# Output product of a SoLU layer after talking-heads attention: seven block products per pair of token tiles for eight

## The chip, the core and the metric

The kernel runs on one core of one Trainium2 chip. The metric is the device time of one execution in microseconds (us); lower is better. The engines are TensorE (PE, with its weight loads PEld), VectorE (DVE), ScalarE (ACT), GpSimd (POOL) and SyncE (SP, which here only issues DMAs). Each engine works through its own instructions in order and waits on semaphores for the others.

## The reference

Attention with mixing across heads gives `x` of 1792 tokens by 768; the layer behind it is what the change touches:

```python
def _moe_ref(x, w_in, w_out, g_ln):          # x 1792x768, w_in 768x1024, w_out 1024x768
    h = x @ w_in
    e = np.exp(h - np.max(h, axis=-1, keepdims=True))
    solu = h * (e / (np.sum(e, axis=-1, keepdims=True) + 1e-09))
    mu = np.mean(solu, axis=-1, keepdims=True)
    var = np.mean((solu - mu) ** 2, axis=-1, keepdims=True)
    ln = (solu - mu) / np.sqrt(var + 1e-06) * g_ln
    return (ln @ w_out).astype(np.float32)
```

`w_in` and `w_out` arrive as 64-bit floats.

## The kernel before

The first 440 us are attention; the change leaves them alone. Every product in f32 accuracy is made of f16 parts: a value is scaled and split into a high and a low f16 part, and a product is three f16 products, high by high, high by low and low by high.

The second stage works on 14 tiles of 128 tokens (`NT`), in the order of `TURNS`. For a tile `t`:

- `hidden` (line 984) makes `x @ w_in` on PE in 36 matmuls of 512 columns, into one of three pairs of PSUM banks. Tile `t` needs the banks of tile `t - 3`, which are free after `solu_product` of that tile. Tile 0 is made at the end of attention.
- The SoLU chain runs on DVE, ACT and POOL: `solu_max` (DVE, line 1508, reads PSUM), `solu_exp` (ACT, 1519), `solu_guard` and `solu_invert` (DVE, 1530 and 1533, one column), `solu_product` (DVE, 1536, reads PSUM and SBUF), `ln_mean` (DVE, 1547), `ln_square` (ACT, 1552), `ln_var` (DVE, 1558), `ln_root` (POOL, 1563, one column), `ln_newton` (DVE, four small steps, 1568 to 1578), `ln_apply` (POOL, 1584, 1024 columns), `ln_hi` (ACT, 1590) and `ln_lo` (POOL, 1594).
- `turn` (line 1598) turns each half of the layer norm's rows by a DMA transpose on SP, from SBUF to SBUF, so that tokens lie along the columns.
- `project` (line 1609) multiplies the turned tile with `wo_h` and `wo_l`, in two halves of 384 output columns with 8 x 3 matmuls each, 48 in all. `emit` (ACT, 1621) scales each half out of PSUM, and SP stores it (1765).

`w_out` is prepared beside this. Its eight blocks of 128 rows are fetched as 64-bit words (`fetch_w_out`), made f32 by `convert_steps` (DVE 898, 904, 909 and 914, ACT 901, POOL 917) and their largest value found (ACT 1478). When all eight are there, one factor for all is worked out (DVE, ending in `gs_wo`, line 1490), and each block is split: `w_out_hi` on ACT (line 360) and `w_out_lo` on DVE (line 365).

The order on each engine is set by `Plan`: each task has engines with costs, tasks that it follows, a due time and rings of buffers, and a list scheduler takes what is ready and due first. For `w_out` block `kc` the due time is `9.0 * kc`, and `project` of a tile is due eleven tiles after its `hidden` (`LAG`). So one `project` stands between `hidden` of tile 12 and of tile 13, and all others behind the last `hidden`.

Of the kernel before, what the change touches and what calls it, by code (L numbers as in the profile page):

```python
# [240 lines left out]
def kernel(  # L241
# [1159 lines left out]
    with tc.manual_schedule():  # L1401
# [43 lines left out]
        junk = wt_p.tile([128, DFF], F32, name="junk")  # L1445
# [154 lines left out]
        ENDS = [[0, DM // 2, DM] if t < NT - 1 else [0, 2 * DM // 3, DM] for t in range(NT)]  # L1600

        def project(t, n, kcs):
            c0, c1 = ENDS[t][n : n + 2]
            if kcs[0] == 0:
                y = (ps_x, ps_y)[n].tile([128, 512], F32, tag="x", name=f"y{n}_{t}")
                ys[t, n] = y[:, 0 : c1 - c0]
            for kc in kcs:
# [8 lines left out]

        def emit(t, n):
            if n == 0:
                outs[t] = h_p.tile([128, DM], F32, tag="o", name=f"o_{t}")
# [67 lines left out]
        for t in range(NT):  # L1687
# [33 lines left out]
            for i, z in enumerate("hl"):  # L1721
                add(
                    ("zT", t, z),
                    one(turn, t, z),
                    {"sp": 1.4},
                    after=[("zl" if z == "h" else "zo", t)],
                    behind=[("zT", t - 1, z)] if t else [],
                    due=T + 9.5 + 2 * i,
                    ring="t" + z,
                    until=[("zP", t, 0, KFF - 1), ("zP", t, 1, KFF - 1)],  # L1730
                    dma=(16, 262, 16.4),
                )
            T = 7.75 * (t + LAG)
            for n in range(2):
                parts = [[kc] for kc in range(KFF)] if t == 0 else [list(range(KFF))]
                before = [("zP", t - 1, n, KFF - 1)] if t else []
                for j, kcs in enumerate(parts):
                    add(
                        ("zP", t, n, kcs[-1]),
                        one(project, t, n, kcs),  # L1740
                        {"pe": (ENDS[t][n + 1] - ENDS[t][n]) / 384 * 0.488 * len(kcs)},
                        after=[("zT", t, "h"), ("zT", t, "l")] + [("zL", kc) for kc in kcs],
                        behind=before,
                        due=T + (3.9 * n if t else 0.9 * j + 0.45 * n),
                        ring=None if j else "XY"[n],
                        until=[("zE", t, n)],
                    )
# [55 lines left out]
```

## Time and profile before

| | |
|---|---|
| three timed runs | 650.59, 653.63, 655.91 us; median 653.63 us |
| span of the profiled execution | 657.9 us |
| PE busy | 632.8 us, 96% of the span |
| DVE busy | 475.1 us, 72% |
| ACT busy | 451.0 us, 69% |
| POOL busy | 280.1 us, 43% |
| matmuls of `project`, line 1609 | 672, from 536.6 us to the last start at 653.4 us |

The profile is one execution; its span of 657.9 us is the only time that it has of its own, and lies 4.3 us above the median of the timed runs. A matmul's duration in it contains the time in which it overlaps with its neighbours, so what a row of matmuls costs is read from the distance of their starts. Times in the trace are microseconds from the start of the span; "idle before" is how long the engine waited before an instruction, with the instruction that ended the wait.

### The profile page before, as it was taken

The numbers are of one execution on the slowest core, as the hardware profiler recorded it, in microseconds if no ns is written. First come the engines' busy times: TensorE is split into PE (matmuls) and PEld (weight loads), VectorE is DVE, ScalarE is ACT, GpSimd is POOL, SyncE is SP. The second block draws the span as 40 slices with busy tenths as digits, with TensorE's granted clock in tenths as the row PEclk, the third lists the DMA queues.
The fourth block names the chain that finished last, engine by engine and source line by source line (L and its number), as shares of the span: only waits on it lengthen the run. The fifth ranks groups of instructions, "written<-read, shape, count | busy, mean of one in ns | idle before, by whom it ended". The sixth has DMA issues, their size and how long they took to land.

```text
span 657.9 us, 17741 instructions
## 1 busy us (share of the span) xinstructions
PE 632.8 (96%) x6660; PEld 433.7 (66%) x6660; DVE 475.1 (72%) x1314; ACT 451.0 (69%) x981; POOL 280.1 (43%) x427
## 2 busy tenths in 40 slices
PE   6889999999999999999899999999999999999997
PEld 6647767777767778778677777774444455666664
DVE  5769998879997689997699999849889896100000
ACT  4679888989888898988799997725455576311111
POOL 2025683235844254593254246404666846300000
PEclk9779999999999999999899999999999999999999
DMA  9037578467677448788746763019964422541211
GB/s 242 12 133 229 178 152 178 156 196 221 204 185 169 150 140 236 234 175 206 219 154 221 214 224 119 3 41 295 186 160 112 97 48 57 113 113 51 64 55 48
DMA packets 114029, 98.53 MB, mean 150 GB/s; under 512 B 69604, under 2 KB 104600, under 8 KB 113944
## 3 DMA queue, kind: packets, MB, share of 16 engines
q1 hardware_dynamic: 108120, 83.62, 45.8%
q0 software_dynamic: 4416, 12.40, 6.9%
q10 hardware_dynamic: 1408, 1.38, 0.8%
q8 instruction: 52, 0.85, 0.5%
q14 instruction: 33, 0.27, 0.1%
HBM read 33.24 MB, written 9.63 MB: 65 GB/s over the span
## 4 chain that ended last, share of the span: by engine, by line
PE 64%; DVE 17%; ACT 7%; DMA 4%; issue 3%; POOL 2%; SPq 1%; ACTq 0%; DVEq 0%; POOLq 0%
PE y L1609 17%; PE po L766 15%; PE ps_h L984 12%; PE px L815 7%; PE ps L644 6%; PE pm L711 6%; DVE dead L721 4%; DVE s L661 3%; ACT e L737 3%; ACT s L656 2%; DMA raw_q<-in_q_dram 2%; DVE hl_k L365 1%; ACT p_t L369 1%; DMA sr<-s 1%; DMA cv_wi<-in_moe_w_in_dram 1%
## 5 line engine op out<-in xcount | busy, mean ns | idle before, releaser
L766 PE MATMUL po<-wr,e 128*112 128x120 f32 x1440 | 176.0, 273 | 6.4 <-POOL wr L758 4.9
L766 PEld LDWEIGHTS po<-wr,e 128*112 128x112 f32 x1440 | 156.8, 178 | 36.8 <-POOL wr L758 15.9
L758 POOL TENSOR_SCALAR wr<-wq,sm 128x120 f32<-128x120 f32 x180 | 77.1, 436 | 186.1 <-DVE sm L752 90.6
L737 ACT ACTIVATE e<-pm,nb,c_exp 128x448 f32<-128x448 f32 x180 | 131.4, 734 | 19.6 <-DVE dead L721 10.2
L721 DVE TENSOR_SCALAR_CACHE_REDUCE dead<-pm,c_nexp 128x448 f16<-128x448 f32 x180 | 121.7, 676 | 14.1 <-PE pm L711 10.1
L661 DVE SCALAR_TENSOR_TENSOR s<-ps,s 120x448 f16<-120x448 f32 (+1 forms) x192 | 112.2, 615 | 16.1 <-ACT s L656 13.8
L369 ACT COPY p_t<-po 112x480 f32<-112x480 f32 x180 | 108.2, 625 | 13.7 <-PE po L766 12.3
L656 ACT ACTIVATE s<-ps 120x448 f16<-120x448 f32 (+1 forms) x192 | 97.3, 552 | 18.1 <-PE ps L644 17.5
L815 PE MATMUL px<-p_t,raw_v 112*64 112x120 f32 (+3 forms) x1632 | 86.8, 259 | 0.8 <-ACT e L737 0.7
L815 PEld LDWEIGHTS px<-p_t,raw_v 112*64 112x64 f32 x1632 | 76.1, 137 | 16.0 <-issue 11.4
L984 PE MATMUL ps_h<-wi,xf 128*128 128x512 f16 x396 | 86.0, 379 | 0.2 <-DVE u L1536 0.2
L644 PE MATMUL ps<-k,q 64*64 64x448 f16 (+2 forms) x1008 | 79.7, 359 | 2.2 <-DVE s L661 1.5
L1609 PE MATMUL y<-wo_h,lth 128*128 128x384 f16 (+2 forms) x224 | 73.0, 326 | 0.0
L1609 PE MATMUL y<-wo_l,lth 128*128 128x384 f16 (+2 forms) x224 | 73.0, 326 | 0.0
L1609 PE MATMUL y<-wo_h,ltl 128*128 128x384 f16 (+2 forms) x224 | 73.0, 326 | 0.0
L984 PEld LDWEIGHTS <-xf 128*128 128x128 f16 x396 | 38.8, 98 | 46.8 <-issue 0.4
L1621 ACT ACTIVATE o<-y,c_out 128x384 f32<-128x384 f32 (+2 forms) x28 | 16.2, 579 | 72.7 <-PE y L1609 72.7
L1609 PEld LDWEIGHTS <-lth 128*128 128x128 f16 x448 | 43.8, 98 | 29.3
L711 PE MATMUL pm<-sr,wp_hi 64*64 64x448 f16 x720 | 57.1, 363 | 4.4 <-DMA sr<-s 2.4
L644 PEld LDWEIGHTS <-q 64*64 64x64 f16 (+2 forms) x1008 | 34.7, 107 | 24.4 <-issue 8.0
L1594 POOL TENSOR_TENSOR ll<-u,lh 128x1024 f16<-128x1024 f32 x14 | 31.4, 2245 | 15.1 <-ACT lh L1590 9.0
L737 ACT ACTIVATION_READ_ACCUMULATOR e<-pm,nb,c_exp 128x1 f32 x180 | 37.6, 209 | 0.0
(182 smaller groups left out, 800.1 us busy)
## 6 DMA issues: line engine op xcount, KB each, us to landing
sr<-s SPq DMA_DIRECT2D x176, 210.0 KB
cv_wi<-in_moe_w_in_dram SPq DMA_DIRECT2D x24, 256.0 KB
cv_wo<-in_moe_w_out_dram SPq DMA_DIRECT2D x8, 768.0 KB
raw_k<-in_k_dram POOLq DMA_DIRECT2D x18, 224.0 KB, 3.7
raw_q<-in_q_dram POOLq DMA_DIRECT2D x18, 224.0 KB, 5.4
raw_v<-in_v_dram POOLq DMA_DIRECT2D x18, 224.0 KB, 3.8
xh<-xsh SPq DMA_DIRECT2D x9, 224.0 KB
xl<-xsl SPq DMA_DIRECT2D x9, 224.0 KB
```

The lines of the kernel that those rows point to most:

```text
L369: nc.scalar.copy(out=out, in_=in_)
L644: nc.tensor.matmul(sps[b, c, h + e][lo:hi], q2[b, g][rows, 2 * j + x, i0 + lo : i0 + hi], k1[b, g][rows, 2 * j + y], start=(a == 0), stop= ...
L656: nc.scalar.activation(out=s_t[b, c][0 : y.shape[0], h, 0], in_=y, func=AF.Copy, scale=2.0**-E_S)
L661: nc.vector.scalar_tensor_tensor(out=t[:, h, 1], in0=y, scalar=2.0**-E_S, in1=t[:, h, 0], op0=ALU.mult, op1=ALU.subtract)
L711: nc.tensor.matmul(pmx[b, u + i][64 * e : 64 * e + 64, 0:S], w[rows], sr[b, u][rows, e, z], start=(a == 0), stop=(a == 2),)
L721: nc.vector.tensor_scalar(out=dead, in0=pmx[b, u][:, 0:S], scalar1=c_nexp[0:UK, b : b + 1], scalar2=None, op0=ALU.mult, op1=ALU.min, accum ...
L737: nc.scalar.activation(out=ee[b, u], in_=pmx.pop((b, u))[:, 0:S], func=AF.Exp, bias=nbs.pop((b, u)), scale=c_exp[0:UK, b : b + 1], accum_o ...
L758: ENG[eng].tensor_scalar(out=w, in0=wq[0:UK, 0 : H * UN], scalar1=sm, scalar2=1.0, op0=ALU.mult, op1=ALU.mult)
L766: nc.tensor.matmul(ps[:, c * 120 : (c + 1) * 120], e[:, c * CP : (c + 1) * CP], w, start=True, stop=True)
L815: nc.tensor.matmul(xps[b, blk, g][e * 64 : e * 64 + 64, i, cut], raws["v", b, p][:, e, c * D : (c + 1) * D], next(x for y, x in block_view ...
L984: nc.tensor.matmul(ps[:, n], xx[:, kc, o : o + 128], ww[:, kc, n * 512 : (n + 1) * 512], start=(kc == 0 and a == 0), stop=(kc == KDM - 1 a ...
L1609: nc.tensor.matmul(ys[t, n], lts[t, x][:, kc], w[:, kc, c0:c1], start=(kc == 0 and a == 0), stop=(kc == KFF - 1 and a == 2),)
```

## The change

One level of Strassen's algorithm on the product with `w_out`. Two token tiles form a pair: with the turned rows of a pair as a 2 by 2 of blocks (two tiles by two halves of the 1024 inner rows) and `w_out` as a 2 by 2 (two halves of the rows by two halves of the columns), seven block products replace eight. The form with shared sums is used (Winograd's): four sums of blocks on each side.

- `w_out`: all blocks are first scaled in place (`w_out_scale`), four sums of 384 columns are made for each of four pairs of blocks (`w_out_sum`), and what is split is 20 pieces instead of 8: the eight blocks, four double sums (`tt`, 768 columns) and eight single ones (384 columns). `w_out_lo` becomes a plain subtraction (line 1510) that the scheduler may put on DVE or POOL, and so do the sums. Block `kc` is due at `7.0 * kc`, and the fetches have four buffers for two.
- Layer norm: `ln_store` writes both halves of a tile's rows to DRAM, and `turn` transposes them from DRAM.
- Pair 0 is projected plainly (`project` with `i == 0`, 4 steps of 24 matmuls). For pairs 1 to 6, high and low parts are added up again to f32 (`pair_whole`, line 1660, two of 1024 columns), four sums are made (`pair_sum`, 1673, four of 512 columns), and split again (`part_hi` on ACT, 1678, and `part_lo`, 1510, two of 1024 columns each). `project` then has 7 steps of 12 matmuls of 384 columns. Steps 0 to 2 read the turned tiles, steps 3 to 6 the split sums.
- `emit` leaves ACT for the pairs, except step 0: DVE adds each block product from PSUM to what is there (line 1755), nine instructions a pair.
- All 14 `hidden` come before the first step of `project`.

```diff
-        lt_p = ctx.enter_context(tc.tile_pool(name="lt", bufs=9))
+        lt_p = ctx.enter_context(tc.tile_pool(name="lt", bufs=2))
+        sz_p = ctx.enter_context(tc.tile_pool(name="sz", bufs=2))
...
-        LAG = 11
+        ln_dr = [dram.tile([NT, 128, DFF], F16, name=f"ln_{z}") for z in "hl"]
...
-        def w_out_lo(kc):
-            split_lo(wo_l[:, kc], wo_raw[kc // 4][:, kc % 4], gs_wo[:, kc : kc + 1], wo_h[:, kc])
+        def w_out_scale(kc, eng):
+            x, s = raw_of(kc), gs_wo[:, kc : kc + 1]
+            if eng == "act":
+                nc.scalar.activation(out=x, in_=x, func=AF.Copy, scale=s)
+            else:
+                ENG[eng].tensor_scalar(out=x, in0=x, scalar1=s, scalar2=1.0, op0=ALU.mult, op1=ALU.mult)
+
+        def minus(eng, out, x, y):
+            ENG[eng].tensor_tensor(out=out, in0=x, in1=y, op=ALU.subtract)
...
+            out, x, y = ((t[:, 0], b12, b11), (t[:, 1], b22, t[:, 0]), (b21, b21, t[:, 1]), (b12, b22, b12))[i]
+            minus(eng, out, x, y)
...
+        def w_out_hi(k):
+            x, hi, _ = w_out_views(k)
+            nc.scalar.copy(out=hi, in_=x)
+
+        def w_out_lo(k, eng):
+            x, hi, lo = w_out_views(k)
+            minus(eng, lo, x, hi)
...
+        def ln_store(t, z, e):
+            QUEUE[e].dma_start(out=ln_dr["hl".index(z)][t], in_=lns[t, z])
+
+        def turn(i, t, z):
+            if i not in lts:
+                lts[i] = lt_p.tile([128, 2, 2, KFF, 128], F16, tag="lt", name=f"lt_{i}")
+            z = "hl".index(z)
+            nc.sync.dma_start_transpose(out=lts[i][:, z, t], in_=ln_dr[z][2 * i + t])
...
+            h, l = (lts[i][:, z, t].rearrange("p k f -> p (k f)") for z in range(2))
+            ENG[eng].tensor_tensor(
+                out=xs[i][:, 2 * t : 2 * t + 2].rearrange("p n f -> p (n f)"), in0=h, in1=l, op=ALU.add
+            )
...
+        def part_lo(i, t, eng):
+            hi, lo = (szs[i][:, z, 2 * t : 2 * t + 2] for z in range(2))
+            minus(eng, lo, xs[i][:, 2 * t : 2 * t + 2], hi)
...
+            for k in range(KH):
+                wh, wl = factor(j, k)
+                for a, (z, w) in enumerate(((0, wh), (0, wl), (1, wh))):
                     nc.tensor.matmul(
...
+                        ys[i, j],
+                        operand(i, j, z, k),
+                        w,
+                        start=(k == 0 and a == 0),
+                        stop=(k == KH - 1 and a == 2),
...
+                3: lambda: [(py, py), (px, px)],
+                4: lambda: [(c(1, 0), py), (c(1, 1), px)],
...
+            for dst, x in work[j]():
+                nc.vector.scalar_tensor_tensor(out=dst, in0=y, scalar=c_out, in1=x, op0=ALU.mult, op1=ALU.add)
...
-            due = 9.0 * kc
+            due = 7.0 * kc
...
+                    {"dve": 0.48, "pool": 0.95},
...
+                    {"dve": 1.15, "pool": 2.2},
```

The order on DVE just behind the factor of `w_out` (`gs_wo`), before. `u_8522` is the SoLU of tile 11, `wo_l` the low parts of `w_out`:

```order
L1490 TENSOR_SCALAR gs_wo<-g_sb,p_wo 128x8
L1491 TENSOR_SCALAR c_out<-p_wo 128x1
L1558 TENSOR_SCALAR v_8517<-sq_8462,ch 128x1
L1547 TENSOR_SCALAR nmu_8519<-su_8468 128x1
L1508 TENSOR_SCALAR u_8522,nb_8523<-ps_h_7620,ch 128x1024
L365 SCALAR_TENSOR_TENSOR wo_l<-wo_7704,gs_wo,wo_h 128x768 x3
L1568 TENSOR_SCALAR z_8535<-y_8525,v_8517 128x1
```

The same place after; `u_8383`, `u_8465` and `u_8524` are tiles 9, 10 and 11, and `tt` is a sum of blocks of `w_out`:

```order
L1493 TENSOR_SCALAR gs_wo<-g_sb,p_wo 128x8
L1494 TENSOR_SCALAR c_out<-p_wo 128x1
L1577 RECIPROCAL sm_8394<-sm_8394 128x1
L1580 SCALAR_TENSOR_TENSOR u_8383,su_8457<-ps_h_7315,sm_8394,u_8383 128x1024
L1591 TENSOR_SCALAR nmu_8462<-su_8457 128x1
L1552 TENSOR_SCALAR u_8465,nb_8466<-ps_h_7622,ch 128x1024
L1510 TENSOR_TENSOR wo_l<-wo_7710,wo_h 128x768
L1510 TENSOR_TENSOR wo_l<-wo_8009,wo_h 128x768
L1510 TENSOR_TENSOR wo_l<-wo_7710,wo_h 128x768
L1602 TENSOR_SCALAR v_8482<-sq_8478,ch 128x1
L1510 TENSOR_TENSOR tt_8484<-wo_7710 128x384
```

The factor stands one `solu_max` and two `solu_product` earlier in the queue, and what follows it is a longer list: between it and the first split sums of pair 1, DVE has 10 subtractions of 768 columns, 16 of 384, one addition of 1024 and four of 512, beside the chains of tiles 9 to 13.

The order on POOL at the same place, before (`ll` is `ln_lo`, `u` by `rs,nm` is `ln_apply`, `y` by `half_p` is `ln_root`):

```order
L1594 TENSOR_TENSOR ll_8435<-u_8205,lh_8384 128x1024
L1584 TENSOR_SCALAR u_8308<-u_8308,rs_8426,nm_8430 128x1024
L1594 TENSOR_TENSOR ll_8458<-u_8308,lh_8448 128x1024
L1563 TENSOR_TENSOR y_8525<-v_8517,half_p 128x1
L1584 TENSOR_SCALAR u_8432<-u_8432,rs_8538,nm_8540 128x1024
```

After, `u_8314` being tile 8 and `u_8383` tile 9:

```order
L1628 TENSOR_SCALAR u_8314<-u_8314,rs_8402,nm_8404 128x1024
L1507 TENSOR_SCALAR wo_8009<-wo_8009,gs_wo 128x768
L1507 TENSOR_SCALAR wo_7710<-wo_7710,gs_wo 128x768
L1640 TENSOR_TENSOR ll_8475<-u_8314,lh_8468 128x1024
L1607 TENSOR_TENSOR y_8528<-v_8482,half_p 128x1
L1628 TENSOR_SCALAR u_8383<-u_8383,rs_8538,nm_8542 128x1024
L1510 TENSOR_TENSOR tt_8484<-wo_8009,tt_8484 128x384
L1510 TENSOR_TENSOR wo_l<-wo_7710,wo_h 128x768
L1640 TENSOR_TENSOR ll_8563<-u_8383,lh_8548 128x1024
```

Into the chain of the tiles on POOL come six scalings of 768 columns, six sums of 384, two low parts of 768 and two of 384, and one `pair_whole` of 1024 columns. The `ln_root` of tile 13 stands behind all of these, and behind `ln_lo` of tiles 8 to 12.

The order on DVE where the first split sums of pair 1 are made, after (`xs` are the pair's f32 blocks and sums, `sz` the split ones, `u_8747` is tile 13; none of this is in the kernel before):

```order
L1673 TENSOR_TENSOR xs_8825<-xs_8825 128x512
L1602 TENSOR_SCALAR v_8861<-sq_8840,ch 128x1
L1673 TENSOR_TENSOR xs_8825<-xs_8825 128x512 x3
L1612 TENSOR_SCALAR z_8887<-y_8882,v_8861 128x1
...
L1622 TENSOR_SCALAR nm_8893<-nmu_8838,rs_8891 128x1
L1510 TENSOR_TENSOR sz_8867<-xs_8825,sz_8867 128x1024
L1755 SCALAR_TENSOR_TENSOR o_8912<-y_1_8869,c_out,xs_8825 128x384
L1510 TENSOR_TENSOR sz_8867<-xs_8825,sz_8867 128x1024
L1755 SCALAR_TENSOR_TENSOR xs_8825<-y_2_8897,c_out,xs_8825 128x384
```

The last `sz` row here is what PE's step 3 of pair 1 waits for; the Newton steps of tile 13, which need POOL's `ln_root`, stand ahead of it.

## Rows read from the trace of the kernel before

**Rows 1.** The page, part 1: busy time, share of the span, instructions.
```profile
PE 632.8 (96%) x6660; PEld 433.7 (66%) x6660; DVE 475.1 (72%) x1314; ACT 451.0 (69%) x981; POOL 280.1 (43%) x427
```

**Rows 2.** Timeline of PE: start us, us, engine, line, operation, count [idle before].
```profile
458.26 70.09 PE L984 MATMUL ps_h<-wi,xf 128*128 128x512 f16 x324
...
528.80 7.93 PE L984 MATMUL ps_h<-wi,xf 128*128 128x512 f16 x36 [0.22 <-DVE u L1536]
...
544.36 7.93 PE L984 MATMUL ps_h<-wi,xf 128*128 128x512 f16 x36
```

**Rows 3.** The chain that ended last, its end: start us, us, what.
```profile
527.45 1.30 DVE u L1536 x2
528.80 7.93 PE ps_h L984 x36
536.73 7.80 PE y L1609 x48
544.53 7.77 PE ps_h L984 x36
552.30 101.41 PE y L1609 x624
```

**Rows 4.** Busy time by stretch: length, PE, PEld, DVE, ACT, POOL, PEclk, DMA, GB/s.
```profile
444.40:532.30 87.90, 87.68 (x408) 39.86 (x407) 77.00 (x165) 48.45 (x75) 55.92 (x35) 1.00 0.69 166
532.30:553.00 20.70, 20.70 (x111) 10.67 (x110) 17.09 (x38) 14.51 (x20) 12.03 (x8) 1.00 0.24 49
```

**Rows 5.** Timeline of DVE, four places.
```profile
457.46 2.37 DVE L909 TENSOR_SCALAR cv_wo<-cv_wo 128x768 uint32<-128x768 uint32 x1
...
502.26 1.28 DVE L1536 SCALAR_TENSOR_TENSOR u<-ps_h,sm,u 128x1024 f32<-128x1024 f32 x1
...
532.20 0.23 DVE L1490 TENSOR_SCALAR gs_wo<-g_sb,p_wo 128x8 f32<-128x8 f32 x1
...
533.78 2.87 DVE L365 SCALAR_TENSOR_TENSOR wo_l<-wo,gs_wo,wo_h 128x768 f16<-128x768 f32 x3
...
537.50 5.50 DVE L365 SCALAR_TENSOR_TENSOR wo_l<-wo,gs_wo,wo_h 128x768 f16<-128x768 f32 x5
```

**Rows 6.** Timeline of POOL, at those places and later.
```profile
457.17 2.23 POOL L1594 TENSOR_TENSOR ll<-u,lh 128x1024 f16<-128x1024 f32 x1 [1.32 <-ACT lh L1590]
...
461.21 1.85 POOL L917 TENSOR_TENSOR wo<-cv_wo 128x768 f32<-128x768 f32 x1
...
525.68 1.20 POOL L1584 TENSOR_SCALAR u<-u,rs,nm 128x1024 f32<-128x1024 f32 x1
528.04 2.14 POOL L1594 TENSOR_TENSOR ll<-u,lh 128x1024 f16<-128x1024 f32 x1 [1.16 <-ACT lh L1590]
...
537.76 3.51 POOL L1584 TENSOR_SCALAR u<-u,rs,nm 128x1024 f32<-128x1024 f32 x1 [4.53 <-DVE nm L1578]
...
561.46 0.55 POOL L1563 TENSOR_TENSOR y<-v,half_p 128x1 f32<-128x1 f32 x1 [2.07 <-DVE v L1558]
```

**Rows 7.** Groups by line: duration ns min/median/max, first and last start (SPq: time of issue).
```profile
L909 DVE TENSOR_SCALAR cv_wo<-cv_wo x8: 549/566/2373, 449.7 to 518.9; 128x768 uint32<-128x768 uint32 x8
L1508 DVE TENSOR_SCALAR_CACHE_REDUCE u<-ps_h,ch x14: 1268/1274/1284, 444.4 to 553.3; 128x1024 f32<-128x1024 f32 x14
L1536 DVE SCALAR_TENSOR_TENSOR u<-ps_h,sm,u x14: 1283/1284/1286, 447.5 to 558.3; 128x1024 f32<-128x1024 f32 x14
...
L1598 SPq DMA_TRANSPOSE lth<-lh x14: 1232/1233/2027, 461.8 to 583.4; - x14
```

**Rows 8.** Timeline of DVE: the small steps of one tile.
```profile
557.00 0.27 DVE L1568 TENSOR_SCALAR z<-y,v 128x1 f32<-128x1 f32 x1 [1.37 <-POOL y L1563]
557.31 0.15 DVE L1571 TENSOR_SCALAR z<-z 128x1 f32<-128x1 f32 x1
557.50 0.27 DVE L1574 TENSOR_SCALAR rs<-z,ch,y 128x1 f32<-128x1 f32 x1
557.80 0.21 DVE L1578 TENSOR_SCALAR nm<-nmu,rs 128x1 f32<-128x1 f32 x1
557.93 0.14 DVE L1530 TENSOR_SCALAR sm<-sm 128x1 f32<-128x1 f32 x1
558.11 0.16 DVE L1533 RECIPROCAL sm<-sm 128x1 f32<-128x1 f32 x1
```

**Rows 9.** Busy time by stretch near the start (columns as in rows 4).
```profile
8.00:16.00 8.00, 4.22 (x80) 3.74 (x74) 4.30 (x12) 3.78 (x8) 0.00 (x0) 1.00 1.14 256
16.00:24.00 8.00, 7.33 (x62) 5.97 (x64) 4.68 (x14) 4.78 (x12) 0.00 (x0) 0.57 0.16 41
```

More of the change, by code (lines that the diff above doesn't have):

```diff
@@ L1444 @@
         half_p = wt_p.tile([128, 1], F32, name="half_p")
[L1445 removed]
+        junk = wt_p.tile([128, DFF], F16, name="junk")
         wo_raw, wo_steps = [], {}
@@ new lines, in pair_sum, with part_hi @@
+        def pair_sum(i, j, eng):
+            a11, a12, a21, a22 = (xs[i][:, n] for n in range(4))
+            out, x, y, op = (
+                (a22, a21, a22, ALU.add),
+                (a21, a11, a21, ALU.subtract),
+                (a11, a22, a11, ALU.subtract),
+                (a12, a12, a11, ALU.subtract),
+            )[j]
+            ENG[eng].tensor_tensor(out=out, in0=x, in1=y, op=op)
+        def part_hi(i, t):
+            if i not in szs:
+                szs[i] = sz_p.tile([128, 9 * FH], F16, tag="sz", name=f"sz_{i}")[:, 0 : 8 * FH].rearrange("p (z n f) -> p z n f", z=2, n=4)
+            nc.scalar.copy(out=szs[i][:, 0, 2 * t : 2 * t + 2], in_=xs[i][:, 2 * t : 2 * t + 2])
@@ L1720 @@
                 prev = [(n, t)]
-            for i, z in enumerate("hl"):
+            for z, n, d in (("h", "zl", 9.3), ("l", "zo", 11.5)):
                 add(
[L1723 to L1731, printed above, removed]
-                )
@@ L1733 @@
[L1733 to L1737, printed above, removed]
-                    add(
[L1739 to L1746, printed above, removed]
-                    )
-                    before = [("zP", t, n, kcs[-1])]
-                add(
-                    ("zE", t, n),
-                    one(emit, t, n),
-                    {"act": (ENDS[t][n + 1] - ENDS[t][n]) / 384 * 0.35 + 0.15},
-                    after=before,
-                    behind=[("zE", t, n - 1)] if n else [("zE", t - 1, 1)] if t else [],
-                    due=T + 4 + 4 * n,
-                    ring=None if n else "o",
-                    until=[("zS", t, 1, i) for i in range(len(stores(t, slice(0, DM))))],
-                )
-                if n == 0 and t < NT - 1:
-                    continue
-                cut = slice(*ENDS[t][n : n + 2]) if t == NT - 1 else slice(0, DM)
-                for i, (_, d, rows) in enumerate(stores(t, cut)):
-                    add(
-                        ("zS", t, n, i),
-                        lambda e, d=d, rows=rows, t=t, cut=cut: nc.sync.dma_start(out=d, in_=outs[t][rows, cut]),
-                        {"sp": 0.6},
-                        after=[("zE", t, n)],
-                        due=T + 8.5 + 0.1 * i,
@@ new lines @@
+                    ("zS", t, z),
+                    lambda e, t=t, z=z: ln_store(t, z, e),
+                    {"sp": 0.6},
+                    after=[(n, t)],
+                    behind=[("zS", t - 1, z)] if t else [],
+                    due=T + d,
+                    dma=(16, 262, 18.5),
+                )
+        NPP = NT // 2
+        STEPS = [(0, j) for j in range(4)] + [(i, j) for i in range(1, NPP) for j in range(7)]
+        chunks = lambda t: range(len(stores(t, slice(0, DM))))
```

254 lines of the change are left out of this document (220 added, 34 removed).

## Prediction

> **What bounds the kernel now.** I read the busy times first: PE has 96% of the span, DVE 72%, ACT 69%, POOL 43% [rows 1]. Where an engine is that full, the next view is its timeline in the stage that the change touches. From 458.3 us `hidden` of tiles 3 to 11 runs without a gap (324 matmuls, so one tile's 36 take 7.77 us), then tile 12 from 528.80, one `project`, tile 13 from 544.36 [rows 2]. The chain that ended last says the rest: 48 matmuls of `project` take 7.80 us, and from 552.30 the other 624 run 101.41 us without a break to 653.7 [rows 3]. So 672 matmuls of 384 columns cost 109.2 us, 0.1625 us each, and 4.2 us pass from the last of them to the end of the span. PE sets the end.
>
> But the chain also steps aside to DVE: `solu_product` of tile 9 at 527.45 precedes `hidden` of tile 12, which waited 0.22 us for it [rows 2, 3]. DVE is busy 77.0 of the 87.9 us up to the factor of `w_out` at 532.2, and POOL 55.9 [rows 4]. PE is full because DVE is just fast enough, and in this stage the change gives DVE and POOL more work.
>
> **What PE saves.** After the change `project` has 4 steps of 24 matmuls and 42 of 12, 600 for 672: 72 times 0.1625, or 11.7 us. If PE never waits, it leaves `hidden` at 544.4 (without the 7.8 us of `project` now in between), ends pair 0 at 560.0 (96 matmuls, 15.6 us), and reaches step 3 of pair 1 at 565.8 (three steps of 1.95). Behind that start lie 39 steps, 76.1 us, and the end of 4.2 us: 646.1 against 657.9.
>
> **What must be there for step 3 of pair 1.** This is the first step that reads split sums. Before, nothing of the kind existed: `project` of tile 0 needed only turned rows eleven tiles old. Now the end is the time D at which the second split sum of pair 1 is done, plus 80.3 us, if D is later than 565.8. Everything turns on D.
>
> *The start of the list.* The factor ended at 532.2 with 11 `solu_max`, 11 `solu_product` and 9 sets of Newton steps ahead of it. In the new order it stands one `solu_max` (1.27) and two `solu_product` (1.28 each, with 0.3 of small steps) earlier [rows 5, 7, 8]: 4.6 us, so about 527.6, and the `solu_product` of tile 9 behind it ends at 529.0. POOL then is where it was at 526.9 to 528, at the end of `ln_apply` of tile 8 [rows 6].
>
> *DVE's list from 529.0.* Operations of this form, `tensor_tensor` on two f32 tiles in SBUF, the trace does not show on DVE at this size. The nearest row is the old `w_out_lo`, also two SBUF inputs: three of 768 columns in 2.87 us, 0.96 each, or 1.25 ns a column [rows 5]. By it 768 columns cost 0.96, 384 cost 0.49, 512 cost 0.64 and 1024 cost 1.28. The two ends: at half of it (a faster mode, as the one-input L909 of 768 columns has with 0.55 [rows 7]) and at that value; I take that value, since it has two inputs as these have. Then 10 x 0.96, 16 x 0.49, 4 x 0.64 and 1.28 are 21.3 us, and the two split sums 2.6. Beside these stand four `solu_max` and four `solu_product`, 10.2 us, five sets of small steps at about 1.6 us (0.9 and 0.3 as shown, two more of 0.2) [rows 8], 8.0, and one `emit` of 384 columns from PSUM, 0.5 by the share of 1.28 us. Sum 42.6: D would be 571.6 if DVE never waited.
>
> *POOL's list from 528.* Undisturbed durations: `ln_root` 0.55, `ln_apply` 1.20, `ln_lo` 2.14, a product of 768 columns 1.85 [rows 6]. From the first scaling to `ln_root` of tile 13 there are 5, 4 and 5 of these three: 2.8 + 4.8 + 10.7. New are six scalings of 768 columns (three quarters of 1.20, 0.9 each, 5.4), six sums of 384 (half of 1.85, 5.5), two low parts of 768 (three quarters of 2.14) and two of 384, 4.8, and `pair_whole` at 2.1. Sum 36.1 us: alone it would end at 564 and hide behind DVE.
>
> *They do not run beside each other.* At 457.46 DVE's L909 took 2.37 us, where the shortest took 0.55: POOL's `ln_lo` had run since 457.17 and ended at 459.40, and L909 ended 0.43 us later. At 537.76 POOL's `ln_apply` took 3.51 us for 1.20, while DVE went through five `w_out_lo` [rows 5 to 7]. `solu_max` and `solu_product`, which read PSUM, stay within 16 ns and 3 ns in all 14 tiles, whatever POOL does [rows 7]. So a POOL operation and a DVE operation on SBUF alone exclude each other, with about 0.1 us gained at a change of hands.
>
> The Trainium skill states this as a rule, on the page "SBUF — State Buffer", section "SBUF: two separate sides": the pair of ports that VectorE and GpSimd share is "an exclusive lock, not a bandwidth split", against VectorE operations with two SBUF inputs or in a two-port mode. The trace agrees, with the 2.37 us for 0.55 above. By that rule the two lists below add up; by separate ports only the longer would count. The time would be 663.0 us by the one and 647.6 by the other.
>
> *The sum.* `ln_root` of tile 13 ends POOL's 36.1 us, and the Newton steps of tile 13, which wait for it, stand ahead of the split sums. Before them all of DVE's 21.3 us on SBUF must have passed too. 36.1 + 21.3 = 57.4, less some 25 changes of hands at 0.1, 54.9: from 528 to 583. Then the Newton steps 0.9, two split sums 2.6 and the `emit` between them 0.5: D = 587. PE ends at 587 + 76.1 = 663.1, the span at 667.3. That is 9.4 us over 657.9. Put on the median of 653.6, the forecast is **663.0 us**, slower by 1.4%.
>
> **The rest.** The closer fetches of `w_out` (7 us a block for 9) bring about one and a half conversions in front of `solu_product` of tile 6, which ended at 503.5 and for which `hidden` of tile 9 began at 504.9 [rows 2, 5]: by 6.5 us more of DVE work PE waits some 5 us there. These are not added, because the later wait for D contains them. Also inside it: `emit` of pair 0 stands on ACT behind casts that wait for POOL's `ln_apply`, so that steps 2 and 3 of pair 0 find their bank taken. The change of `junk` and of the exponents costs nothing. The transposes from DRAM are not in the trace; those from SBUF cost 1.23 us of issue each on SP [rows 7], four for a pair. Pair 2's stand behind the store of tile 12 and before `ln_lo` of tile 12's store, and are needed one pair later. I take 0; at 2 us a transpose more, pair 2 waits up to 8 us, partly under D. Past D, a pair costs DVE 2.6 + 2.6 + 2.6 us and nine `emit` of 0.5, 12.3 us, against 13.65 us of PE: it holds, with POOL nearly done. Were it not to hold, PE would wait for the bank that the last `emit` frees, and behind PE's waiting step stand all later ones.
>
> **Rivals.**
> - *A, the two engines do pass each other.* If the subtractions on DVE exclude POOL less than L909 and L365 do, D is DVE's own list, 571.6, and the end 651.9: 6.0 us less, 647.6 us. For it: these are other opcodes; against it: rows 5 and 6. Not slower, and it decides from D below 577.6.
> - *B, PE keeps its pace.* With `tensor_tensor` at half of L365's price (21.3 falls to 10.7) and no exclusion D falls to 560, below 565.8: 11.7 us less, 641.9 us. Against it: DVE's 87.6% busy with less work.
> - *C, PE loses its clock as well.* After 8 us in which PE was busy for 4.22, the granted clock is 0.57, between its levels of 1.2 and 2.4 GHz [rows 9]; later it is 1.00 throughout. Between 553 and 587 PE would have 21 us of work in 34. If 16 us of steps after D run at the lower level, they take 32: not all at once, but +8 and more, 671 us.
>
> **How the numbers follow.** What can be told from no change here is 1%, 6.5 us either way (647.1 to 660.1); the timed runs spread 5.3. The forecast has 0.55: its own range is 655 to 670, as D moves by 4 us with the start of the list and by 3 with the handovers; about a fifth of it is within 1%. A has 0.20, on the lower bound, half and half. B has 0.10. C has 0.15. Faster 0.10 + 0.10 = 0.20; same 0.10 + 0.12 = 0.22; slower 0.58. The range leaves out B and the far part of C: 646 to 675.
>
> **What would show it.** PE's steps of pair 1 should start 15 us and more after the last `hidden`'s natural time, with idle time before L1722 put down to DVE's L1510 or to ACT's L1736; step 3 of pair 1 at about 587. L1510 on DVE should spread between 0.9 and 2.9 us at 768 columns, and POOL's L1628 and L1507 likewise, in that stage. From pair 2 on PE should run at 13.65 us a pair. The forecast is wrong if step 3 of pair 1 starts before 578, if L1510 at 768 columns stays near 0.9, or if a later pair takes over 14.5 us.

## Result, and the profile after

The changed kernel takes 663.29 us (median of four runs, 658.11 to 664.53), the kernel before 652.36 us (four runs, 650.59 to 655.91): 1.015 times as long, with a 95% interval of 1.0101 to 1.0198. The forecast was 663.0 us.

The page, part 1, and the end of the chain that ended last. PE is busy for 8 us less than in [rows 1], in a longer span; the last 22 steps run at 43.07 / 264 x 12 = 1.958 us, so PE sets the end again:

```profile
PE 624.8 (94%) x6588; PEld 425.3 (64%) x6588; DVE 570.6 (86%) x1428; ACT 460.2 (70%) x989; POOL 316.7 (48%) x449
...
614.50 43.07 PE y L1722 x264
```

The timeline of PE, which answers to [rows 2]. Where `hidden` ran without a gap there are waits for `solu_product` (L1580), and `project` waits four times for `emit` on ACT (L1736, L1739). Step 3 of pair 1 starts at 577.68 with two matmuls that read only the high parts; the first that reads a low part starts at 578.67. Behind it, in pair 2, PE waits for DVE:

```profile
451.84 46.78 PE L984 MATMUL ps_h<-wi,xf 128*128 128x512 f16 x216
500.74 15.70 PE L984 MATMUL ps_h<-wi,xf 128*128 128x512 f16 x72 [2.12 <-DVE u L1580]
516.49 15.70 PE L984 MATMUL ps_h<-wi,xf 128*128 128x512 f16 x72
534.43 9.60 PE L984 MATMUL ps_h<-wi,xf 128*128 128x512 f16 x36 [2.24 <-DVE u L1580]
...
554.51 0.32 PE L1711 MATMUL y<-wo_h,lt 128*128 128x384 f16 x1 [2.67 <-ACT o L1736]
...
561.82 0.32 PE L1711 MATMUL y<-wo_h,lt 128*128 128x384 f16 x1 [1.56 <-ACT o L1736]
...
570.25 0.32 PE L1722 MATMUL y<-wo_h,lt 128*128 128x384 f16 x1 [2.43 <-ACT o L1736]
...
574.61 0.32 PE L1722 MATMUL y<-tz_h,lt 128*128 128x384 f16 x1 [2.25 <-ACT xs L1739]
...
577.68 0.53 PE L1722 MATMUL y<-tz_h,sz 128*128 128x384 f16 x1
...
578.67 0.55 PE L1722 MATMUL y<-tz_h,sz 128*128 128x384 f16 x2
...
593.31 0.32 PE L1722 MATMUL y<-tz_h,sz 128*128 128x384 f16 x1 [0.38 <-DVE o L1755]
...
594.45 0.50 PE L1722 MATMUL y<-tz_h,sz 128*128 128x384 f16 x2 [0.65 <-DVE sz L1510]
```

The timeline of DVE: the factor of `w_out` and the second split sum of pair 1, the prediction's D, which ends at 578.62:

```profile
518.83 0.71 DVE L1493 TENSOR_SCALAR gs_wo<-g_sb,p_wo 128x8 f32<-128x8 f32 x1
...
576.92 1.70 DVE L1510 TENSOR_TENSOR sz<-xs,sz 128x1024 f16<-128x1024 f32 x1
```

Groups by line, with durations in ns (min/median/max), as in [rows 7]: subtractions in SBUF spread by a factor of three at 768 columns (0.95 to 2.89 us) and of more than four at 384 (0.54 to 2.48), and POOL's `ln_apply` by two, while `solu_max`, which reads PSUM, stays within 18 ns:

```profile
L1510 DVE TENSOR_TENSOR wo_l<-wo,wo_h x11: 544/953/2889, 522.3 to 564.8; 128x768 f16<-128x768 f32 x7, 128x384 f16<-128x384 f32 x4
L1510 DVE TENSOR_TENSOR wo<-wo,tt x3: 544/1450/2482, 537.1 to 558.8; 128x384 f32<-128x384 f32 x3
...
L1552 DVE TENSOR_SCALAR_CACHE_REDUCE u<-ps_h,ch x14: 1265/1272/1283, 438.0 to 559.9; 128x1024 f32<-128x1024 f32 x14
...
L1628 POOL TENSOR_SCALAR u<-u,rs,nm x14: 1182/1634/2545, 448.1 to 575.5; 128x1024 f32<-128x1024 f32 x14
```

How long attention takes differs between executions, so all that follows is counted from the first matmul of the `hidden` of tile 3: 458.26 us before [rows 2], 451.84 after. From there the kernel before takes 199.6 us to the end of the span, the changed one 210.0, which is 10.4 more. From the prediction's prices PE needs 187.4 after the change (11 `hidden` 85.7, pair 0 15.6, 42 steps 81.9, the end 4.2), so it loses 22.6 us: 6.5 in `hidden`, some 13 from there to D, some 3 behind it.

### The profile page after: what moved, and what is told of

It is laid out like the page before. It is cut to its first block, busy times and chain, and to the rows that moved or that the text cites. A ratio compares the mean times of both kernels' runs of the same rounds, so it can differ in the third digit from the quotient of the medians.

```text
span 661.8 us, 17824 instructions
## 1 busy us (share of the span) xinstructions
PE 624.8 (94%) x6588; PEld 425.3 (64%) x6588; DVE 570.6 (86%) x1428; ACT 460.2 (70%) x989; POOL 316.7 (48%) x449
## 5 line engine op out<-in xcount | busy, mean ns | idle before, releaser
L661 DVE SCALAR_TENSOR_TENSOR s<-ps,s 120x448 f16<-120x448 f32 (+1 forms) x192 | 112.3, 616 | 15.4 <-ACT s L656 14.8
L369 ACT COPY p_t<-po 112x480 f32<-112x480 f32 x180 | 108.5, 627 | 10.7 <-PE po L766 9.5
L984 PE MATMUL ps_h<-wi,xf 128*128 128x512 f16 x396 | 87.8, 384 | 4.4 <-DVE u L1580 4.4
L644 PEld LDWEIGHTS <-q 64*64 64x64 f16 (+1 forms) x1008 | 34.3, 107 | 25.0 <-issue 8.4
L1722 PEld LDWEIGHTS <-sz 128*128 128x128 f16 x288 | 28.1, 98 | 22.2 <-issue 2.1
L711 PE MATMUL pm<-sr,wp_lo 64*64 64x448 f16 (+1 forms) x360 | 36.0, 351 | 0.0
L1678 ACT CAST sz<-xs 128x1024 f16<-128x1024 f32 x12 | 12.5, 1044 | 32.1 <-DVE xs L1673 25.6
L1722 PEld LDWEIGHTS <-lt 128*128 128x128 f16 x216 | 21.4, 99 | 19.9 <-issue 6.4
L365 DVE SCALAR_TENSOR_TENSOR xsl<-px,x_sc,xsh 128x120 f16<-128x120 f32 (+1 forms) x96 | 26.0, 326 | 8.0 <-ACT xsh L360 8.0
```

The lines of the kernel that those rows point to most:

```text
L369: nc.scalar.copy(out=out, in_=in_)
L644: nc.tensor.matmul(sps[b, c, h + e][lo:hi], q2[b, g][rows, 2 * j + x, i0 + lo : i0 + hi], k1[b, g][rows, 2 * j + y], start=(a == 0), stop= ...
L661: nc.vector.scalar_tensor_tensor(out=t[:, h, 1], in0=y, scalar=2.0**-E_S, in1=t[:, h, 0], op0=ALU.mult, op1=ALU.subtract)
L711: nc.tensor.matmul(pmx[b, u + i][64 * e : 64 * e + 64, 0:S], w[rows], sr[b, u][rows, e, z], start=(a == 0), stop=(a == 2),)
L984: nc.tensor.matmul(ps[:, n], xx[:, kc, o : o + 128], ww[:, kc, n * 512 : (n + 1) * 512], start=(kc == 0 and a == 0), stop=(kc == KDM - 1 a ...
L1722: nc.tensor.matmul(ys[i, j], operand(i, j, z, k), w, start=(k == 0 and a == 0), stop=(k == KH - 1 and a == 2),)
```

## Experiments

Each kernel of the table was timed beside the kernel before, in groups on different chips, so its time is given as a multiple of the kernel before's. The program of its own and the repeat of the kernel before have one execution each. D is the end of the last split sum of the first pair that needs them; D and the end are counted from the first matmul of tile 3 and come from one profiled execution. Two of these executions lie well below the median of their kernel's runs: that of "before, blocks every 7 us" (659.4 us for 662.4) and that of "pair 1 plain, every 9 us, five buffers" (650.7 for 653.0).

| kernel | time as a multiple of before's (95%) | D, us | end, us |
|---|---|---|---|
| before | | | 199.6 |
| changed | 1.0150 (1.0101 to 1.0198) | 126.8 | 210.0 |
| new work off POOL | 1.0168 (1.0140 to 1.0196) | 127.1 | 210.1 |
| before, blocks every 7 us | 1.0175 (1.0157 to 1.0194) | | 208.3 |
| changed, blocks every 9 us | 1.0064 (1.0039 to 1.0090) | 122.5 | 206.6 |
| `ln_apply` on ACT | 1.0045 (1.0017 to 1.0073) | 121.4 | 203.1 |
| the last two together | 1.0135 (1.0107 to 1.0164) | 125.9 | 209.0 |
| pair 1 plain | 1.0121 (1.0100 to 1.0143) | 132.9 | 206.2 |
| pair 1 plain, `ln_apply` on ACT | 1.0080 (1.0057 to 1.0102) | 133.4 | 204.3 |
| pair 1 plain, every 9 us, five buffers | 1.0005 (0.9988 to 1.0023) | 131.1 | 200.2 |
| the same, `ln_apply` on ACT | 1.0044 (1.0028 to 1.0061) | 133.1 | 202.1 |
| the same without, waits taken away | 0.9976 (0.9951 to 1.0001) | 127.5 | 198.4 |

### Do the two engines exclude each other?

A program of its own, whose phases are:

```diff
+        (["two"] * 12, ["two"] * 6, 0), (["two"] * 12, ["one"] * 6, 0), (["one"] * 12, ["two"] * 6, 0),
+        (["bank"] * 12, ["two"] * 6, 0), (["bank"] * 12, ["one"] * 6, 0), ([], ["two"] * 6, 12), (["two"] * 12, [], 12),
```

> This program computes nothing of the reference: it runs operations of 768 columns on DVE, POOL and ACT on tiles of its own, first each engine alone (8, 6 or 8 in a row), then two engines at once (12 on DVE or ACT beside 6 on POOL), and writes a constant. 'two' is a subtraction of two f32 tiles in SBUF, 'one' a scaling of one f32 tile in SBUF, 'bank' a scalar_tensor_tensor that reads one operand from PSUM. Theory (the two engines exclude each other when both read SBUF alone): 12 DVE 'two' beside 6 POOL 'two' take about the sum, 12 x 0.95 + 6 x 1.6 = 21 us, or 19 with 0.1 gained at each change of hands; so do 'two' beside POOL's 'one' (11.4 + 5.4 = 17) and 'one' beside POOL's 'two'; DVE 'bank' beside POOL and ACT beside POOL or DVE take only the longer of the two, with the durations they have alone. Rival A (they pass each other): every pair takes the longer of the two, 11.4 us for 12 DVE 'two', with no duration over 1.1 us on DVE.

The timeline of DVE: 12 'two' beside 6 'two' of POOL, beside 6 'one' of POOL, 12 'one' beside 6 'two', 12 'bank' beside 6 'two', and 12 'two' beside ACT.

```profile
61.05 20.76 DVE L47 TENSOR_TENSOR do<-dx,dy 128x768 f16<-128x768 f32 x12 [8.40 <-ACT dx L45]
82.64 14.89 DVE L47 TENSOR_TENSOR do<-dx,dy 128x768 f16<-128x768 f32 x12 [0.83 <-ACT dx L45]
98.42 15.97 DVE L50 TENSOR_SCALAR do<-dx 128x768 f16<-128x768 f32 x12 [0.89 <-ACT dx L45]
115.28 11.87 DVE L51 SCALAR_TENSOR_TENSOR do<-ps,dx 128x768 f16<-128x768 f32 x12 [0.89 <-ACT dx L45]
...
157.92 11.88 DVE L47 TENSOR_TENSOR do<-dx,dy 128x768 f16<-128x768 f32 x12 [18.02 <-ACT dx L45]
```

And POOL's: six 'two' alone, beside DVE's 'two', and beside DVE's 'bank'.

```profile
21.04 11.19 POOL L47 TENSOR_TENSOR po<-px,py 128x768 f16<-128x768 f32 x6 [20.60 <-ACT px L45]
...
61.35 14.68 POOL L47 TENSOR_TENSOR po<-px,py 128x768 f16<-128x768 f32 x6 [17.24 <-ACT ax L45]
...
115.48 11.23 POOL L47 TENSOR_TENSOR po<-px,py 128x768 f16<-128x768 f32 x6 [4.48 <-ACT ax L45]
```

Beside each other, 'two' and 'two' take 20.76 us, where 11.88 (beside ACT) and 11.19 (alone) make 23.07: the sum, less 2.31. The two engines take turns while POOL has work, one operation each, and the gain is some 0.4 us for each of the six turns; the five DVE operations behind POOL's last take what they take alone. With an operand in PSUM both engines take what they take alone, and ACT is in nobody's way. The exclusion is shown, and rival A of the prediction falls. A 'two' on DVE that starts beside a POOL operation ends 0.8 us behind the end of that operation, whether it is a 'two' (1.80 us alone) or a 'one' (0.83). It is as the Trainium skill has it ("SBUF — State Buffer", section "SBUF: two separate sides"): a lock for one whole instruction, not a share of a rate.

### The new work taken off POOL

```diff
-{"act": 0.83, "pool": 1.16}
+{"act": 0.83}
-{"dve": 0.48, "pool": 0.95}
+{"dve": 0.48}
-{"dve": 0.95 * w, "pool": 1.75 * w}
+{"dve": 0.95 * w}
...
```

> The changed kernel with the new work taken off POOL: the scalings of w_out on ACT alone, all sums and low parts on DVE alone; POOL keeps the layer norm's three. Exclusion theory: 17.8 us leave POOL's part of the shared list and 7.1 us come to DVE's, so the sum falls by 10.7 us; but DVE's own list from the factor on, 42.6 + 7.1 = 49.7 us, is now about as long as the sum. The second split sum of pair 1, 59 us behind the factor in the changed kernel, comes 50 to 53 us behind it, and the time falls from 663 to 654 to 658 us. Rival (the two pass each other, DVE's own list decides): DVE's list is 7.1 us longer, the split sums come 66 us behind the factor, 670 us.

1.0168 against 1.0150: no change. Neither side was right. (Of each line above only the engines with their costs are shown.) PE's waits, and DVE's list:

```profile
538.27 10.63 PE L984 MATMUL ps_h<-wi,xf 128*128 128x512 f16 x36 [5.68 <-DVE u L1580]
...
577.51 0.50 PE L1722 MATMUL y<-tz_h,sz 128*128 128x384 f16 x1 [7.16 <-DVE sz L1510]
```

```profile
519.26 0.70 DVE L1493 TENSOR_SCALAR gs_wo<-g_sb,p_wo 128x8 f32<-128x8 f32 x1
...
548.02 2.89 DVE L1510 TENSOR_TENSOR tz_l<-tt,tz_h 128x768 f16<-128x768 f32 x1
...
577.96 1.21 DVE L1510 TENSOR_TENSOR sz<-xs,sz 128x1024 f16<-128x1024 f32 x1
```

The four waits for `emit` are gone, PE waits 7.16 us for the split sum instead, and the end is where it was: those waits were inside the wait for D, as the prediction had it. From the factor to D it is 59.2 us, in the changed kernel 59.1. Adding up DVE's timeline (an operation that took over 0.2 us more than the shortest of its form is counted as lengthened by the difference), the 59.1 us are 40.6 of DVE's own, 14.4 of lengthening and 4.1 idle; here 47.4, 10.4 and 1.4. Every lengthened operation had one of POOL beside it. So the end of the list is DVE's own work, the part of POOL's that happens to meet it, and a few us of waits. In the changed kernel POOL has some 38 us of its own there and lengthens DVE by 14.4; the rest of it lies beside `solu_max`, `solu_product` and the small steps, which it does not touch. Here POOL has half as much, 19.3 us, and still lengthens DVE by 10.4.

### The closer fetches, alone and taken back

```diff
-            due = 9.0 * kc
+            due = 7.0 * kc
```

in the kernel before, and the reverse in the changed one.

> The kernel before with only the blocks of w_out due every 7 us instead of every 9. The prediction said that this brings 6.5 us of conversions in front of solu_product of tile 6 and that hidden of tile 9 then waits some 5 us (the changed kernel's trace shows 2.1 us), which the later wait hid. Here nothing hides it: 2 to 5 us slower than before, 654.5 to 657.5 where before is 652.4. Rival (the wait came from other work of the change, or is made up by the earlier low parts): within 1 us of before.

> The changed kernel with the blocks of w_out due every 9 us again, as before. Theory (DVE has work without a pause up to the last split sum of pair 1, and its whole work sets when that is done; where the conversions stand in it matters little): hidden of tile 9 no longer waits 2.1 us, the factor comes later, the split sums come within 3 us of where they did, and the time is 660 to 666 us. Rival (the closer fetches themselves are the loss, as in the run with them alone, 11.5 us): 652 to 655 us.

Alone, this line costs 1.75%, more than twice what was expected and as much as the whole change. The timeline of PE:

```profile
449.44 39.01 PE L984 MATMUL ps_h<-wi,xf 128*128 128x512 f16 x180
489.61 7.93 PE L984 MATMUL ps_h<-wi,xf 128*128 128x512 f16 x36 [1.15 <-DVE u L1536]
503.00 17.78 PE L984 MATMUL ps_h<-wi,xf 128*128 128x512 f16 x72 [5.46 <-DVE u L1536]
```

Two waits for `solu_product` make 6.6 us, and the 72 matmuls behind them took 2.1 us more than 15.7: 8.7 us in this execution, 11.5 by the medians. Taken back in the changed kernel, the line gives back 0.9%, between the theory (none) and its rival (all). `hidden` then runs without a gap, and D comes 4.3 us earlier although the factor comes 5.8 us later (72.8 for 67.0 us):

```profile
522.39 0.23 DVE L1493 TENSOR_SCALAR gs_wo<-g_sb,p_wo 128x8 f32<-128x8 f32 x1
...
570.55 1.61 DVE L1510 TENSOR_TENSOR sz<-xs,sz 128x1024 f16<-128x1024 f32 x1
```

From tile 3 to D the lengthening of DVE's operations falls from 27.6 to 19.7 us, although POOL's own work there falls only from 78.8 to 76.0; DVE's idle time grows from 9.5 to 11.7. That the order of the conversions changes how often DVE and POOL meet is what the sums show; why these meet less often was not taken apart.

### `ln_apply` on ACT, and the kernel before once more

```diff
-            nc.gpsimd.tensor_scalar(
-                out=u, in0=u, scalar1=sc[t, "rs"], scalar2=sc[t, "nm"], op0=ALU.mult, op1=ALU.add
-            )
+            nc.scalar.activation(out=u, in_=u, func=AF.Identity, bias=sc[t, "nm"], scale=sc[t, "rs"])
```

> The changed kernel with ln_apply (1024 columns, 14 times) on ACT in place of POOL. POOL loses 16.8 us of work that collides with DVE, 6.0 us of it between the factor and the first split sums; ACT gets 14.7 us. Theory (DVE's list plus the part of POOL's time that collides with it, so far 16.4 of 36.1 us): the split sums come 3 to 6 us earlier, 657 to 660 us. Rival A (the collisions are no cost on the path, DVE waits for other things): 663 us, or more because ACT's casts and emits come later.

> The changed kernel with two edits at once: blocks of w_out due every 9 us, and ln_apply on ACT. Alone they brought the last split sum of pair 1 forward by 4.2 us and by 5.3 us, counted from the first matmul of hidden of tile 3. Theory (that moment plus 80.3 us is the end): both together bring it 8 to 10 us forward, and the end comes 199 to 202 us behind that matmul, against 199.6 before: within 0.5% of before, 2 to 5 us under either edit alone. Rival (both edits remove the same waits): no better than ln_apply on ACT alone, 655 us.

> The kernel before, profiled once more. The first profile had a span of 657.9 us where the timed runs since then lie at 649 to 652. Theory (that execution lost time in attention, ahead of the part that the change touches): the 396 matmuls of hidden from tile 3 on start some 8 us earlier than 458.26, and from there to the end of the span it takes 199.6 us again, within 0.5. Rival (the part behind it varies): the start is the same and the rest is shorter.

The kernel before repeats: the 324 matmuls start at 451.18, and it is 199.6 us from there to the end of a span of 650.8. The first profile lost 7 us in attention.

`ln_apply` on ACT brings D forward by 5.4 us and the time to 1.0045, the theory's numbers and a little more. Its mechanism is only part of that: from tile 3 to D POOL's own work falls by 16.4 us and DVE's lengthening by 2.1 (27.6 to 25.5), while DVE's idle time falls by 4.1 (9.5 to 5.4), most of it waits for POOL's `ln_root` and `pair_whole`. Both edits together are worse than either, where the theory expected better and its rival the same as `ln_apply` alone: D at 125.9. The timelines of ACT and DVE show a part of it:

```profile
571.43 1.04 ACT L1676 CAST sz<-xs 128x1024 f16<-128x1024 f32 x1 [3.02 <-DVE xs L1671]
573.15 1.24 ACT L1628 ACTIVATE u<-u,nm,rs 128x1024 f32<-128x1024 f32 x1 [0.67 <-DVE nm L1622]
574.48 1.04 ACT L1634 CAST lh<-u 128x1024 f16<-128x1024 f32 x1
575.43 1.04 ACT L1676 CAST sz<-xs 128x1024 f16<-128x1024 f32 x1
```

```profile
576.50 1.27 DVE L1510 TENSOR_TENSOR sz<-xs,sz 128x1024 f16<-128x1024 f32 x1 [1.26 <-ACT sz L1676]
```

The second cast of the split sums stands behind `ln_apply` and `ln_hi` of tile 13, which wait for DVE; DVE then waits 1.26 us for that cast with the last split sum. The larger part is that DVE's operations lengthen by 24.1 us from tile 3 to D, where they lengthen by 19.7 with the 9 us alone. POOL is busy for 20.5 of the 23 us from 532 to 555, in the changed kernel for 21.5: the planner, which takes the two engines for independent, gives POOL other work in the place of `ln_apply`. Why the two meet more often here was not taken apart.

### Where split sums are needed later

```diff
-        STEPS = [(0, j) for j in range(4)] + [(i, j) for i in range(1, NPP) for j in range(7)]
+        NPL = 2
+        STEPS = [(i, j) for i in range(NPP) for j in range(4 if i < NPL else 7)]
```

> The changed kernel with pair 1 projected plainly too, so that pair 2 is the first to need split sums: 12 matmuls more (1.95 us of PE), and PE has plain work until 31.2 + 5.9 us behind the last hidden, which in the trace of the changed kernel is 581 us, against 578.5 us at which the first pair's split sums were done there. Theory (the one late arrival D costs all): PE hardly waits for split sums; end 581.1 + 32 steps of 1.958 + 4.2 = 648 against 661.8, with 0 to 4 us left of the waits for emit: 649.5 to 653.5 us timed, under or level with the kernel before. Rival (PE's lost time comes from the steps of pairs themselves, emits, banks or clock, not from one arrival): the gain is under 4 us, 660 us or more.

> The changed kernel with ln_apply on ACT and pair 1 projected plainly too. Plain pair 1 alone gave 658.6 us. Theory (fewer collisions help the emits and the tiles' chains as well): 3 to 6 us less than that, 652.5 to 655.5 us, level with before or up to 0.7% slower. Rival (waits for ACT's emits of the plain pairs grow, since ACT has 14.7 us more): 659 us or more.

1.0121 against the changed kernel's 1.0150, which the intervals do not tell apart, and an end 3.8 us earlier in the profiles: a third or so of what the theory said. D is no longer 126.8 but 132.9 here: the transposes of pair 2 wait until PE is done with pair 0's buffer, and DVE waits 3.4 us for ACT's `wo_h` and 0.9 us for a transpose. With `ln_apply` on ACT as well D is not earlier, and the time, 0.8% over before, lies just beyond the 0.7% that the theory allowed. So three more were made:

```diff
-        lt_p = ctx.enter_context(tc.tile_pool(name="lt", bufs=2))
+        lt_p = ctx.enter_context(tc.tile_pool(name="lt", bufs=5))
...
-                lts[i] = lt_p.tile([128, 2, 2, KFF, 128], F16, tag="lt", name=f"lt_{i}")
+                lts[i, t] = lt_p.tile([128, 2, KFF, 128], F16, tag="lt", name=f"lt_{i}_{t}")
```

> The changed kernel with pair 1 plain too, blocks of w_out due every 9 us, and the two buffers of turned pairs cut into five buffers of one turned tile. With pair 1 plain alone the first split sums came 133 us behind the first matmul of hidden of tile 3, where PE needs them at 123, because the turned rows of pair 2 wait for the buffer of pair 0. Theory: with the buffers cut they come 122 to 127 us behind it, and the end, 32 steps and 4.2 us later, 191 to 197 us behind that matmul, 646 to 651 us timed, 0 to 1% faster than before. Rival (the waits for ACT's emits of the plain pairs decide): 655 us or more.

> The kernel of the run before this one with ln_apply on ACT as well. Theory (collisions between POOL and DVE delay DVE's list): the first split sums come early enough that PE hardly waits for them, the end is 190 to 195 us behind the first matmul of hidden of tile 3, 644 to 649 us timed, 0.5 to 1.3% faster than before. Rival (ACT is now full enough that its casts and emits hold PE up, as with ln_apply on ACT and pair 1 plain, which gained nothing over pair 1 plain alone): not under 650 us.

Level with before (1.0005), but with D and the end short of the theory's ranges; with `ln_apply` on ACT worse, as its rival had it. Two waits are left in the first of the two, one of PE and one of DVE:

```profile
546.68 0.48 PE L1712 MATMUL y<-wo_h,lt 128*128 128x384 f16 x1 [4.34 <-ACT o L1738]
```

```profile
566.76 3.58 DVE L1510 TENSOR_TENSOR wo_l<-wo,wo_h 128x384 f16<-128x384 f32 x4 [2.90 <-ACT wo_h L1537]
```

The last kernel removes both:

```diff
+            if i < NPL and j > 1:
+                ys[i, j] = h_banks[(NT + i) % 3][:, j - 2, 0:DH]
...
-            due = 9.0 * kc
+            kc, was = (n + KH) % KFF, (n + KH - 1) % KFF
+            due = 9.0 * n
...
-                    due=due + d,
+                    due=due + d + 16.0 * (i == 3),
```

> The kernel with pair 1 plain, blocks every 9 us and five turned buffers, and what its trace shows PE and DVE waiting for taken away. Steps 2 and 3 of both plain pairs use PSUM banks that hidden has left, so that PE need not wait there for ACT's emit of step 0 (4.5 us, and 1.0 at the lower clock behind it). The blocks of w_out are fetched in the order 4 to 7, 0 to 3, so that the f32 tile of pair 2 takes the buffer that is free first, and the four sums of w_out that overwrite blocks wo_h still needs are due 16 us later (DVE waited 2.9 us for their casts at 566.8 us, with the sums of pair 2 behind). Theory (emit and the first split sums are what is left between PE and its pace): the first split sums come 122 to 127 us behind the first matmul of hidden of tile 3 (131 so far), the end 191 to 195 us behind it (200.2 so far), 0.7 to 1.3% faster than before. Rival (the waits move to the next steps, or the split sums come no earlier): within 0.3% of before.

PE no longer waits in the plain pairs, and D is 3.6 us earlier, but the end only 1.8, short of the theory's 5 to 9. The rival was right: the wait moved to a later step, and the time is within 0.3% of before. What is late next is again `emit` on ACT, of step 0 of pair 2. It stands behind a cast of the split sums, two `emit` of pair 1 and the issue of their stores, while four sums of 512 columns take 6.19 us on DVE, 2.87 in the kernel without these edits:

```profile
576.27 0.48 PE L1726 MATMUL y<-tz_h,lt 128*128 128x384 f16 x1 [4.92 <-ACT xs L1744]
```

```profile
564.93 6.19 DVE L1673 TENSOR_TENSOR xs<-xs 128x512 f32<-128x512 f32 x4
```

0.9976 times before, and the interval (0.9951 to 1.0001) contains 1: perhaps a quarter of a per cent faster, which these runs do not settle.

## Why the prediction was right, and where it was not

The way that the change would go and the moment that decides it, D, were right. That 663.0 came so near to 663.29 is in part luck: of the terms behind it several were wrong and made up for each other.

**PE's saving of 11.7 us** holds where PE does not wait: pairs 4 to 6 take 13.65 us each, seven steps of 1.95. It needs 187.4 us, loses 22.6 and takes 210.0. **The end as D plus 80.3 us** holds with 1.4 to 3.8 us more. In the five kernels in which pair 1 is the first with split sums, D lies between 121.4 and 127.1 and the end 81.7 to 84.1 us behind it; in the changed kernel 83.2, 2.9 more than forecast, from five waits of 0.2 to 0.7 us for DVE, four of them for `emit`. Counted from tile 3, the factor was forecast at 69.3 and came at 67.0 (the terms of its shift add to 4.4, not 4.6), D at 128.7 and came at 126.8, the end at 209.0 and came at 210.0: D was 1.9 early, the rest 2.9 long.

**The prices** held: 768 columns took 0.95 us undisturbed (0.96 taken), 384 0.54 (0.49), 1024 1.22 (1.28); DVE's own list 40.6 us (42.6), POOL's some 38 (36.1). **The exclusion** is shown by the program of its own.

**The sum of the two lists was the first step that failed**, although its number was right. POOL's 36.1 and DVE's 21.3 us on SBUF, less the handovers, made 54.9, with the Newton steps, split sums and `emit` 59 from 528 us on; measured from the factor, 59.1. But that POOL's whole list adds to DVE's is not so: with 17.8 us taken off POOL and 7.1 added to DVE, the sum should have fallen by 10.7, and D stayed. What sets D is DVE's own list, what POOL collides with of it, and some waits: 40.6, 14.4 and 4.1. The 14.4 are some 38% of POOL's time, but that share is no rule: with the work off POOL it is 54% (10.4 of 19.3). Two wrong parts cancelled, which is luck: too much for POOL, and nothing for DVE's 18 us of `solu_max`, `solu_product` and small steps.

**The closer fetches were the second.** "These are not added, because the later wait for D contains them": taken back, they give 5.6 us of the 10.9 by which the changed kernel is slower. The wait of `hidden` of tile 9 is 2.12 us where some 5 were named, and it is contained, but the earlier conversions also delay D, by 4.3 us. In the kernel before, where nothing contains them, they cost 11.5 us where 5 were named.

**`emit` of pair 0 inside the wait** is shown by the run with the new work off POOL; in the changed kernel itself the two arrive together, the first matmul on a low part 0.05 us behind D. **The transposes from DRAM at 0** stay argued: their issue takes 1.3 us at the median and 3.8 at the most, and in the changed kernel no wait of PE or DVE is put down to them, but no run has them alone, and with pair 1 plain DVE waits 0.9 us for one.

**The signs of being wrong.** Of the three, "if step 3 of pair 1 starts before 578": it starts at 577.68, but in an execution whose tile 3 starts 6.4 us earlier than in [rows 2]; counted from there it is 125.8, where 578 is 119.7. The second, "if L1510 at 768 columns stays near 0.9": it does not. The third, "if a later pair takes over 14.5 us", came: pair 2 took 15.4, from 586.91 to 602.33 us, pair 3 14.1, and only pairs 4 to 6 the forecast 13.65. So the step by which DVE keeps up with PE past D failed for pair 2, where PE waited for DVE's `emit` and for a split sum. Rivals A and B fell; C came in part, below.

## What to carry to other kernels

A change that takes work from the bounding engine and gives more to the next ones can move the end to the first thing that needs all of the new work, and it is read as one moment plus what lies behind it. VectorE's and GpSimd's work on SBUF excluded each other here, but only where it met: count VectorE's whole list and the part of GpSimd's time that falls on its SBUF operations. That part does not follow from GpSimd's total (14.4 us of some 38, 10.4 of 19.3), so moving work between the two may give little, above all where a planner takes them for independent. Test a change of a due time by itself: here one line of the change cost as much as all of it.

## What was not expected of the hardware

Taking turns costs the two engines nothing but gains some 0.4 us a turn, two changes of hands, against the sum (20.76 for 23.07 us over six turns); the prediction had 0.1 a change.

TensorE's granted clock fell where PE had waited for two to three microseconds, though not each time. In [rows 4] it stays at 1.00 (earlier in the kernel before it is 0.57 from 36 to 44 us and 0.51 from 320 to 323.5 too, so that "later it is 1.00 throughout" holds only for this stage); in the changed kernel, with columns as there:

```profile
555.00:560.00 5.00, 5.00 (x22) 2.60 (x21) 4.97 (x8) 1.50 (x3) 2.93 (x2) 0.67 0.24 94
560.00:565.00 5.00, 3.44 (x22) 1.98 (x21) 4.93 (x10) 4.66 (x10) 3.39 (x3) 1.00 0.00 0
...
575.00:580.00 5.00, 4.85 (x21) 2.25 (x20) 4.96 (x7) 1.54 (x2) 3.32 (x2) 0.66 0.65 164
```

0.67 follows the wait of 2.67 us that ended at 554.51, and 0.66 those of 2.43 and 2.25 us that ended at 570.25 and 574.61. Behind the wait of 2.24 us that ended at 534.43, tile 13's 36 matmuls took 9.60 us for 7.93. The wait of 2.12 us ahead of 500.74 was followed by no fall. Part of each stretch runs at 1.2 GHz, where a matmul starts every 0.32 us for 0.16. That is a loss of 1 to 2 us each time, nearly all of it ahead of D; rival C had put 8 and more behind D, where the clock is 1.00 again from 580 us on.
